# Order of the first loads, the second token tile's turn, and the first chunk's bias seed in a gated SSM and MLP kernel

## The chip, the cores and the metric

The kernel runs on one core of one Trainium2 chip. The metric is the device time of an execution in microseconds (us). Every execution is listed with its span (first to last instruction, about 1.8 us less than its time); each kernel leaves one profiled execution. Verdicts compare fast executions only: one that is over 1.5% above the fastest of the same kernel is called slow. Each interval is a 95% interval.

## The reference, cut to what matters

```python
x = A_x                                           # 2048 tokens x 640
g = sigmoid((x * gate_w).sum(-1, keepdims=True))
a = ssm(x, ...)                                   # a complex diagonal scan over the tokens
b = gelu(x @ w1 + b1) @ w2 + b2                   # 640 -> 1728 -> 640
out = g * a + (1 - g) * b
```

The kernel takes the tokens in four chunks of 512, each of four tiles of 128. The argument is about the first chunk's `x @ w1`, before everything else can start.

## The kernel before: the parts that matter

```python
load_x0(nc.sync, 0, 1, 0, KA * P)       # token tile 0, first 256 of 640 columns, 64 KB
load_w1a(nc.scalar, 0)                  # "strip 0": rows 0..127 of w1, 768 columns, 192 KB
load_x0(nc.sync, 1, 2, 0, KA * P)
load_w1a(nc.scalar, 1)
load_x0(nc.sync, 2, 3, 0, KA * P)
load_x0(nc.sync, 3, 4, 0, KA * P)
load_w1a(nc.sync, 2)
# ... then, all on SyncE: two transposing loads (columns 256..639), strips 4 and 3, the rest
for n in (512, 512, 512, 512, 512, 128, 128, 128, 128):     # warm-up, L237
    nc.tensor.matmul(pA[:, 0:n], lhsT=ones(P), rhs=ones(n), start=True, stop=True)

def turn_first(a, other):               # TensorE turns a token tile against an identity (L240)
    t = bank()                          # one of 8 PSUM banks
    turn(t, 0, a, 0)
    turned(nc.vector, t, 0, a, 0, 1)    # evict to SBUF (L247 DVE, L249 ScalarE)
    turn(other, a * P, a, 1)
    turned(nc.scalar if a else nc.vector, other, a * P, a, 1, 2)

turn_first(0, pA)
# ...
banks = [bank() for _ in range(FA)]     # 6 banks, one per 128 columns of a strip
# ... three filler matmuls (L363), then part(kd, a) = six 128-column matmuls (L278):
#     strip kd x token tile a, accumulated in the six banks
strip(0, 0, P, True, 0, FA // 2)
turn_first(1, pA)
strip(0, 0, P, True, FA // 2, FA)
part(1, 0)
turn_first(2, pA)
part(0, 1)
part(1, 1)
turn_first(3, pA)
part(0, 2)
# ... part(1,2), part(0,3), part(1,3), then strip 2 (256 columns at a time), strip 4, strip 3 (512)

def last_bank(c):                       # the last 65 columns, seeded with their bias
    p = bank()
    pv = p[:, 0:TPC * NL].rearrange("p (a n) -> p a n", a=TPC)
    if c == 0:
        nc.tensor.matmul(pv, lhsT=ident[:], rhs=b1x..., start=True, ...)     # L294
        return p, pv
    nc.scalar.activation(out=pv, in_=b1x..., func=ACT.Identity)              # L297
    act(0.4)
    return p, pv
```

## Time and profile before

| | before |
|---|---|
| time, median of the first three executions | 215.36 us |
| span of the profiled execution, a fourth one of 214.71 us | 212.9 us |
| TensorE (PE) busy | 208.7 us, 98% |
| DVE / ScalarE busy | 183.5 us / 101.7 us |

The span is one long TensorE stretch. So two things can shorten it: less TensorE work, or an earlier pass through the opening, in which TensorE waits for loads and evictions. The prediction shows the lines.

### The profile page before, as it was taken

Reading aid. Unit: us, or ns where it says so; the run is one execution under the profiler, and the core shown is the slowest. Engines: PE = TensorE matmul, PEld = TensorE weight load, DVE = VectorE, ACT = ScalarE, POOL = GpSimd, SP = SyncE. Lnnn points to the kernel's source line nnn. Section 1 sums busy time; section 2 is a strip of 40 time slices with the busy share of each in tenths; the row PEclk is TensorE's granted clock in tenths of the full one; section 3 lists DMA queues with packets and bytes.
Section 4 is the critical chain, followed back from the end, with each engine's and each line's share of the span. In section 5 each row is a group of like instructions: output and inputs, shape, how many; then the busy total and the mean of one; then the engine's idle time right before and its main releaser. Section 6 shows DMA issues by size and latency. Waiting matters only on the chain.

```text
span 212.9 us, 3594 instructions
## 1 busy us (share of the span) xinstructions
PE 208.7 (98%) x1372; PEld 125.2 (59%) x1383; DVE 183.5 (86%) x336; ACT 101.7 (48%) x182; POOL 62.7 (29%) x101
## 2 busy tenths in 40 slices
PE   8999999999999999999999999999999999999994
PEld 5745444454576644774457777444457587676773
DVE  2589999999989999999999999999999999903153
ACT  3599856665868587203653210456682422205100
POOL 7034079764432462404235503145000000000000
PEclk9999999999999999999999999999999999999999
DMA  6999999996000000061000005100000000100011
GB/s 176 228 218 214 191 237 313 300 211 167 3 0 0 3 0 0 12 186 65 0 0 3 0 20 167 62 0 0 0 5 14 0 3 31 62 34 0 0 66 62
DMA packets 33314, 16.24 MB, mean 76 GB/s; under 512 B 24720, under 2 KB 33296, under 8 KB 33296
## 3 DMA queue, kind: packets, MB, share of 16 engines
q1 hardware_dynamic: 32704, 15.57, 29.1%
q10 hardware_dynamic: 432, 0.43, 0.6%
q8 instruction: 11, 0.18, 0.4%
q14 instruction: 7, 0.06, 0.1%
q0 software_dynamic: 160, 0.01, 0.1%
HBM read 7.48 MB, written 2.62 MB: 47 GB/s over the span
## 4 chain that ended last, share of the span: by engine, by line
PE 97%; DMA 1%; issue 0%; DVE 0%
PE bank L608 27%; PE bank L278 26%; PE bank L667 20%; PE bank L551 20%; DMA xn<-in_A_x_dram 1%; PE bank L624 1%; PE bank L304 1%; PE bank L240 0%; DVE ot L672 0%; PE bank L363 0%; PE bank L294 0%; PE bank L393 0%; PE bank L376 0%
## 5 line engine op out<-in xcount | busy, mean ns | idle before, releaser
L608 PE MATMUL bank<-w_sb,gel 128*128 128x384 bf16 (+1 forms) x416 | 57.9, 299 | 0.0
L608 PEld LDWEIGHTS <-gel 128*128 128x128 bf16 x416 | 40.3, 98 | 17.0 <-issue 0.8
L554 ACT ACTIVATE bu<-bank 128x512 bf16<-128x512 f32 x40 | 23.6, 597 | 37.6 <-PE bank L551 37.6
L283 ACT ACTIVATE gel<-bank,colB 128x512 bf16<-128x512 f32 x52 | 34.0, 693 | 11.0 <-PE bank L278 10.8
L667 PEld LDWEIGHTS <-hs 128*128 128x128 bf16 x330 | 31.7, 98 | 11.6
L515 POOL TENSOR_SCALAR e<-g,cq 128x2 f32<-128x2 bf16 x15 | 18.3, 1222 | 64.3 <-DVE g L508 64.3
L508 DVE TENSOR_TENSOR_SCAN g<-r_c,carry,v 128x512 bf16<-128x512 f32 x30 | 37.2, 1271 | 0.0
L616 ACT ACTIVATE gb<-bank,gcol 128x384 f32<-128x384 f32 (+1 forms) x32 | 15.1, 525 | 33.9 <-PE bank L624 16.9
L278 PE MATMUL bank<-xT,w1a 128*128 128x512 bf16 (+2 forms) x158 | 27.2, 325 | 0.2
L667 PE MATMUL bank<-CT_re,hs 128*128 128x320 bf16 (+2 forms) x165 | 27.1, 295 | 0.0
L667 PE MATMUL bank<-CT_im,hs 128*128 128x320 bf16 (+2 forms) x165 | 27.1, 295 | 0.0
L672 DVE SCALAR_TENSOR_TENSOR ot<-bank,gcol,gb 128x320 bf16<-128x320 f32 (+2 forms) x33 | 17.4, 533 | 9.6 <-PE bank L667 9.5
L551 PE MATMUL bank<-xT,BT_im 128*128 128x512 bf16 x99 | 24.8, 379 | 0.1
L551 PE MATMUL bank<-xT,BT_re 128*128 128x512 bf16 x97 | 24.5, 379 | 0.2
L278 PEld LDWEIGHTS <-w1a 128*128 128x128 bf16 x162 | 14.1, 99 | 11.8
L582 DVE TENSOR_TENSOR bank<-xn,Dbc 128x320 f32<-128x320 bf16 (+2 forms) x33 | 14.5, 483 | 7.1 <-ACT gb L616 7.1
L278 PE MATMUL bank<-xT,w1b 128*128 128x512 bf16 x80 | 17.9, 379 | 0.0
L551 PEld LDWEIGHTS <-BT_im 128*128 128x128 bf16 x100 | 9.8, 98 | 11.8
L517 POOL TENSOR_TENSOR carry<-e,e 128x1 f32<-128x1 f32 x30 | 15.8, 547 | 1.3
L551 PEld LDWEIGHTS <-BT_re 128*128 128x128 bf16 x100 | 9.6, 98 | 11.0
L489 DVE TENSOR_TENSOR v<-wa,wb 128x512 bf16<-128x512 bf16 x40 | 15.2, 422 | 0.6
L597 ACT ACTIVATE bank<-b2bc 128x384 f32<-128x384 bf16 (+1 forms) x24 | 11.7, 529 | 7.1 <-DVE ot L672 7.1
(112 smaller groups left out, 215.8 us busy)
## 6 DMA issues: line engine op xcount, KB each, us to landing
out_dram<-ot SPq DMA_DIRECT2D x15, 160.0 KB, 1.8
w_sb<-in_B_w_dram SPq DMA_DIRECT2D x2, 640.0 KB, 6.0
xn<-in_A_x_dram SPq DMA_DIRECT2D x2, 640.0 KB, 4.3
w_sb<-in_B_w_dram SPq DMA_DIRECT2D x1, 800.0 KB, 8.8
w1b<-in_B_w_dram SPq DMA_DIRECT2D x5, 128.0 KB, 3.4
xn<-in_A_x_dram SPq DMA_DIRECT2D x4, 160.0 KB, 2.8
w1a<-in_B_w_dram SPq DMA_DIRECT2D x3, 192.0 KB, 3.1
w1a<-in_B_w_dram ACTq DMA_DIRECT2D x2, 192.0 KB, 3.0
```

Of the source, the lines that this page charges most:

```text
L278: nc.tensor.matmul(p[:, t0:t1], lhsT=w, rhs=xT[c][:, kd, t0:t1], start=(kd == 0) if first is None else first, stop=(kd == last), skip_grou ...
L283: nc.scalar.activation(out=gel[c][:, kf, :], in_=p[:, :], func=ACT.Gelu_apprx_tanh, bias=b1_c[:, kf:kf + 1])
L489: nc.vector.tensor_tensor(out=o, in0=a, in1=b, op=op)
L508: nc.vector.tensor_tensor_scan(s["g"][:, ri, :], r_c[:, ks:ks + 1].to_broadcast([P, CH]), s["v"][:, ri, :], init, ALU.mult, ALU.add)
L515: nc.gpsimd.tensor_scalar(out=t[:], in0=g[:, :, CH - 1], scalar1=f[:, ks:ks + 1], scalar2=None, op0=ALU.mult)
L517: nc.gpsimd.tensor_tensor(out=carry[:, ri, ks:ks + 1], in0=m[0][:, ri:ri + 1], in1=m[1][:, 1 - ri:2 - ri], op=op)
L551: nc.tensor.matmul(p[:], lhsT=BT[ks >= KSA][:, kd, (ks % KSA if ks < KSA else ks - KSA) * P:][:, 0:P], rhs=xT[c][:, kd, :], start=(kd == 0 ...
L554: nc.scalar.activation(out=bu[:, ri, :], in_=p[:], func=ACT.Identity)
L608: nc.tensor.matmul(p[:, col:col + d1 - d0], lhsT=gel[c][:, kf, a * P:(a + 1) * P], rhs=w2_sb[:, kf, d0:d1], start=False, stop=False, skip_ ...
L616: nc.scalar.activation(out=gbs[ti][:, d0:d1], in_=p[:, col:col + d1 - d0], func=ACT.Identity, scale=gcol[:, 1, ti:ti + 1])
L667: nc.tensor.matmul(p[:, 0:d1 - d0], lhsT=hs[c][:, j, lo:lo + P], rhs=CT[:, j % KS, d0:d1], start=False, stop=(j == 2 * KS - 1), skip_group ...
L672: nc.vector.scalar_tensor_tensor(out=ot[:, d0:d1], in0=p[:, 0:d1 - d0], scalar=gcol[:, 0, ti:ti + 1], in1=gbs[ti][:, d0:d1], op0=ALU.mult, ...
```

## The change

It means to bring the second token tile in together with the first, so that both are turned while TensorE would otherwise wait for an eviction, and to take one matmul off TensorE.

```diff
     load_x0(nc.sync, 0, 1, 0, KA * P)
-    load_w1a(nc.scalar, 0)
-    load_x0(nc.sync, 1, 2, 0, KA * P)
+    load_x0(nc.scalar, 1, 2, 0, KA * P)
+    load_w1a(nc.sync, 0)
     load_w1a(nc.scalar, 1)
-    load_x0(nc.sync, 2, 3, 0, KA * P)
     load_x0(nc.sync, 3, 4, 0, KA * P)
+    load_x0(nc.scalar, 2, 3, 0, KA * P)
     load_w1a(nc.sync, 2)
...
-    def turn_first(a, other):
-        t = bank()
+    def turn_first(a, other, t=None):
+        t = t or bank()
...
-        turned(nc.scalar if a else nc.vector, other, a * P, a, 1, 2)
+        turned(nc.scalar, other, a * P, a, 1, 2)
...
-        if c == 0:
-            nc.tensor.matmul(pv, lhsT=ident[:], rhs=b1x[:]... , start=True, stop=True, ...)
-            return p, pv
...
+    turn_first(1, banks[FA - 1], banks[FA - 2])
     # (three fillers)
-    strip(0, 0, P, True, 0, FA // 2)
-    turn_first(1, pA)
-    strip(0, 0, P, True, FA // 2, FA)
+    part(0, 0)
+    part(0, 1)
     part(1, 0)
     turn_first(2, pA)
-    part(0, 1)
     part(1, 1)
     turn_first(3, pA)
```

Lines move: L277, L299, L359 and L292 of the changed kernel are L278, L304, L363 and L297 of the one before.

More of the change, by code (lines that the diff above doesn't have):

```diff
@@ L292, in last_bank @@
         pv = p[:, 0:TPC * NL].rearrange("p (a n) -> p a n", a=TPC)
-        if c == 0:
-            nc.tensor.matmul(pv, lhsT=ident[:], rhs=b1x[:].rearrange("p (o n) -> p o n", o=1).to_broadcast([P, TPC, NL]),
-                             start=True, stop=True, skip_group_check=True)
-            return p, pv
         nc.scalar.activation(out=pv, in_=b1x[:].rearrange("p (o n) -> p o n", o=1).to_broadcast([P, TPC, NL]), func=ACT.Identity)
```

## The prediction

> **What bounds the kernel now.** I read the page's busy shares first, then its chain of waits, then the chain of the first 20 us in order of time, then the timeline of the first 9 us engine by engine. The page:
>
> ```profile
> PE 208.7 (98%) x1372; PEld 125.2 (59%) x1383; DVE 183.5 (86%) x336; ACT 101.7 (48%) x182; POOL 62.7 (29%) x101
> PE 97%; DMA 1%; issue 0%; DVE 0%
> ```
>
> TensorE is busy for 98% of the span and is 97% of the chain that ends last. DVE, at 86%, has slack: its last `hs` write is at 184.6 us and TensorE starts to read those at 199.2. So a change helps only as far as it takes work off TensorE or lets TensorE get through its opening sooner. Everything that the change moves lies in the opening (before 20 us). The chain there (start, length, what):
>
> ```profile
> 0.72 2.76 DMA xn<-in_A_x_dram
> 3.48 0.05 issue
> 3.53 0.40 PE bank L240 x2
> 3.93 0.32 PE bank L363 x3
> 4.25 0.44 PE bank L278 x3
> 4.68 0.21 PE bank L240 x2
> ...
> 9.15 1.89 PE bank L278 x8
> 11.04 0.01 PE bank L393
> 11.05 6.05 PE bank L278 x28
> 17.11 0.11 PE bank L294
> ```
>
> 2.76 us go to the first token tile's load. From 3.53 us there is always a TensorE piece. L240 turns a token tile, L363 are three filler matmuls, L278 are the strips of the first product, and L294 is the bias seed that the change takes away: 0.11 us of chain. The transfers and evictions behind it (start, length, engine):
>
> ```profile
> 0.72 0.90 ACTq L126 DMA_DIRECT2D w1a<-in_B_w_dram  x2
> 0.72 1.83 SPq L135 DMA_DIRECT2D xn<-in_A_x_dram  x4
> 1.65 1.28 ACT L147 ACT_TABLE_LOAD   x1 [1.65 <-PEq L725]
> 2.60 0.43 SPq L126 DMA_DIRECT2D w1a<-in_B_w_dram  x1
> 3.07 2.65 SPq L150 DMA_TRANSPOSE xT<-in_A_x_dram  x2
> 5.76 1.06 SPq L126 DMA_DIRECT2D w1a<-in_B_w_dram  x2
> ```
>
> Each plain issue takes about 0.47 us of SyncE (four in 1.83 us, with gaps of 0.05), a transpose 1.3. Adding each issue's time to landing to its start gives landings of 3.48 (tile 0), 3.67 (strip 0), 3.86 (tile 1), 4.26 (strip 1), 4.90 (tile 2), 5.70 (tile 3), 6.04 (strip 2), 7.58 (first transpose) and 8.88 (strip 4). Two details of TensorE's records matter. First, its clock: twelve matmuls start in 3.53 to 4.90 us and 44 in the 2.30 us after; successive starts of 128-column matmuls lie 0.107 us apart before 4.90 and 0.056 after. Work that is pulled ahead of 4.90 counts half. Second, two hand-overs further on are set by loads: the first 256-column strip starts at 7.625, 0.127 after the matmul before it instead of 0.056 (the transpose landed at 7.58), and strip 4's weights are loaded at 8.918, just after their landing at 8.88, where TensorE was ready at 8.93. **A gain in the first 4 us is worth nothing unless strip 4 also lands earlier.**
>
> **What the Trainium skill says.** (1) "TensorE: Matmul & The Clock Gate", Part 1: the array starts at half rate and opens after some 4 us of activity (plus or minus 0.5 us), with starts 107 and 56 ns apart. The trace agrees: 0.107 and 0.056, changing at 4.90 us, 4.1 after the first matmul. (2) "DMA: Bandwidth & Descriptors", "Queues, rings and completion order": each DMA engine takes turns between the queues at packet granularity. The packets of the first 3.5 us fit: those of tile 0 (512 bytes, 27 ns each) and of strip 0 (1536 bytes, 65 ns) run interleaved on the two queues. (3) Same page, "Issuing engines are not separate DMA queues": a second issuing engine saves issue time only. So the reorder can bring a transfer forward, but not add bandwidth. (4) "ScalarE: Activation LUTs", "What ACT_TABLE_LOAD costs": 186 ns + 0.833 per column with immediate operands, 403 ns for 260 columns; the trace's three other seeds took 380 to 383 ns.
>
> **Part by part.**
>
> *Loads.* Both queues now open with a token tile. An engine has 8 packets of each (128 rows over 16 engines). Tile 0 shared its turns with strip 0: 8 x (27+65) = 0.74 us; now with tile 1: 8 x (27+27) = 0.43. Tile 0 should land 0.3 us earlier, near 3.2, tile 1 with it (before 3.86). Then strips 0 and 1 share the turns, 8 x (65+65) = 1.04 us, and land together. The four transfers are the same bytes as before, when the last of them landed at 4.26, so I put strip 0 at about 4.2 (before 3.67): **later by half a microsecond.** SyncE issues four loads, not five, ahead of the transposes, so the transposes and strip 4 are issued 0.47 us sooner. DMA engines are about 95% occupied by then, so I expect 0.3 to 0.5 us of it: first transpose near 7.2, strip 4 near 8.5.
>
> *TensorE to 7.2 us.* The warm-up matmuls end at about 3.28 (last start 3.17 + 0.107), which caps the earlier start: turns from 3.28, not 3.53. Four turns and three fillers at 0.107 reach 4.03; the eviction behind the first strip (0.33 from matmul to DVE, 0.29 on DVE, 0.05 hand-over) is ready at 3.95 and hidden, where before it was exposed (3.93 + 0.107 to 4.20 leaves 0.16). The first strip then waits for its weights to about 4.25. By 4.90 that gives 7 + 6.1 = 13.1 matmuls against 12. A lead of 1.1 matmuls is 1.1 x 0.056 = **0.06 us**. With the weights at 4.0 it would be 3 matmuls, 0.17; with 4.4, none.
>
> *Transposes.* If the first lands near 7.2, the **0.07 us** stall at 7.55 goes too; strip 4 is then wanted at 8.80 and lands near 8.5.
>
> *ScalarE.* One more issue pushes its table load from 1.65 to about 2.1; the warm activation ends at 3.6, ahead of its first eviction (about 3.72). Tile 1's second bank is emptied by 4.3, and the sixth strip wants it only at 4.7. DVE has one eviction less.
>
> *Seed.* TensorE loses L294, **0.11 us** from chain (260 columns at 2.4 columns a ns). ScalarE gains 0.38 us here:
>
> ```profile
> 16.79 2.47 ACT L283 ACTIVATE gel<-bank,colB 128x512 bf16<-128x512 f32 x4
> 19.42 0.69 ACT L283 ACTIVATE gel<-bank,colB 128x512 bf16<-128x512 f32 x1 [0.16 <-PE bank L278]
> ```
>
> It works back to back up to 19.26 with 0.16 us to spare. The instruction order puts the seed after the third of the four, so it runs at about 18.5 to 18.9; TensorE needs it at 19.21 - 0.11 - 0.13 = 18.97. That fits by 0.1 us. What follows on ScalarE comes some 0.2 us later, but DVE first needs it at 27.4, and the copies that feed it ended at 23.3.
>
> Sum: 0.06 + 0.07 + 0.11 = 0.24 us, and nothing later takes it back because no TensorE wait shows after 9 us. 215.36 - 0.24 = **215.1 us**.
>
> **Rivals.** *The second token tile buys a wait for strip 0.* If strip 0 lands at 4.5 or later, the head gains nothing and loses about 0.1; only the seed is left: 215.3 to 215.4. For it: strip 0 is now behind two loads and shares with strip 1. Against: the same bytes were in by 4.26. *The head is gained but given back at strip 4.* If its landing stays at 8.88 because the DMA engines are full, everything before 8.93 is lost and the seed alone counts: 215.25. For it: zero slack at 8.93 now. Against: strip 4 is set by issue order (3.1 us from issue to landing), and the transfers move 111 GB/s at 6.8 to 7.3 us, against 278 at 4.8 to 5.3, so the engines are not full of data there. *ScalarE becomes the wait at the first chunk's last tile.* A seed that ends at 19.1 rather than 18.9 gives back 0.1 to 0.2. *All goes well:* strip 0 by 4.0 as well, 0.35 us, 215.0.
>
> **Range and chances.** All of these lie within 0.4 us. The three runs before differ by 0.3, and the clock gate's moment can move by a few tenths. I take 214.75 to 215.5. Two per cent would be 4.3 us, ten times what the opening holds: chances 0.01 faster, 0.98 same, 0.01 slower.
>
> **What would show it.** Tile 0 landing near 3.2 and the first turn at 3.3; first strip near 4.25 with its weights the last to come; starts at 0.107 spacing still up to about 4.9; first 256-column strip with no gap, 0.1 us sooner; strip 4's weights ahead of need; no L294 matmul, and the 65-column matmuls of the first chunk with no gap ahead of them, about 0.24 us sooner than 19.21. A first strip after 4.5, a strip 4 still at 8.9, or a gap before those matmuls would each make the sum wrong by the size given.

## The result, and the profile after

Ratios here are the mean time of one kernel's fast executions over that of the other's of the same rounds, so they are not quite the ratios of the medians that stand beside them. All outputs are right.

In the first measurement the changed kernel took **214.71 us** (median of six, 214.45 to 214.92) and the one before 215.26 us (median of six, 214.71 to 215.46): ratio 0.9976, interval 0.9962 to 0.999. The prediction had 215.1 and 214.75 to 215.5. So the gain was more than twice the 0.24 us foreseen, and the time fell just below the range.

The two profiles do not show such a gain: their spans are 212.93 and 212.80 us (executions of 214.71 and 214.58 us). The page of the changed kernel, its busy line and its chain's:

```profile
PE 208.9 (98%) x1382; PEld 125.0 (59%) x1382; DVE 183.2 (86%) x335; ACT 102.0 (48%) x184; POOL 62.7 (29%) x101
PE 97%; DMA 2%; SPq 0%; DVE 0%; issue 0%
```

(The profile before lacks some ten matmul records, so the counts can't be compared.) The bound is what it was. In the chain of the first 22 us, start and length first, the DMA now waited for is another one:

```profile
1.18 3.30 DMA w1a<-in_B_w_dram
4.48 0.05 issue
4.52 1.18 PE bank L277 x18
5.70 0.11 PE bank L240 x2
5.82 0.34 PE bank L277 x6
6.15 0.27 PE bank L240 x2
```

Before, 2.76 us went to tile 0, and strips began at 4.20. Now the chain comes from strip 0, and strips begin at 4.52, later. The timeline of the same stretch of the changed kernel shows two waits:

```profile
3.27 0.63 PE L240 MATMUL bank<-ident,xn 128*128 128x128 bf16 x4
3.70 0.49 PE L359 MATMUL bank<-const-bfloat16-1.0 128*128 128x128 bf16 x3
4.52 1.18 PE L277 MATMUL bank<-xT,w1a 128*128 128x128 bf16 x18 [0.34 <-DMA w1a<-in_B_w_dram]
5.54 0.28 PE L240 MATMUL bank<-ident,xn 128*128 128x128 bf16 x2
5.65 0.50 PE L277 MATMUL bank<-xT,w1a 128*128 128x128 bf16 x6
5.80 0.29 DVE L247 CAST xT<-bank 128x128 bf16<-128x128 f32 x1 [1.67 <-PE bank L240]
6.14 0.27 PE L240 MATMUL bank<-ident,xn 128*128 128x128 bf16 x2
```

The turns start at 3.27, as soon as the warm-up is over. But after the fillers TensorE has nothing to do until strip 0 lands at 4.48. And there is a wait that nobody had foreseen: the turn of tile 3 (L240 at 6.14) starts 0.21 us after the matmul before it, where a warm start is 0.056 us later. The turn is released by the end of DVE's eviction of tile 2, which runs from 5.80 to 6.09. By the order of the `bank()` calls both tiles are turned in the same PSUM bank; the trace itself leaves bank numbers out. The profile's wait column says nothing there, because pipelined matmul records overlap the gap; it is seen by taking the differences of successive starts.

Strip 4 lands at 8.60 instead of 8.88 and starts at 8.93, as before. So in these two executions the opening is worth nothing, and all but 0.01 of the 0.13 us between them is the seed. The first chunk's end before (L294 is the seed matmul) and after (ScalarE's seed is L292):

```profile
16.94 0.28 PE L294 MATMUL bank<-b1x,ident 128*128 128x260 bf16 x1
17.06 0.81 PE L278 MATMUL bank<-xT,w1c_lo 128*128 128x512 bf16 x3
19.21 0.26 PE L304 MATMUL bank<-w1c_lo,xT 128*128 128x65 bf16 x3
```

```profile
18.56 0.47 ACT L292 ACTIVATE bank<-b1x 128x260 f32<-128x260 bf16 x1
19.09 0.26 PE L299 MATMUL bank<-w1c_lo,xT 128*128 128x65 bf16 x3
```

The seed ends at 19.03; the 65-column matmuls that need it start at 19.09, 0.12 us earlier than before (19.21) and with no gap ahead of them.

### The profile page after: what moved, and what is told of

It reads as the page before. It is cut to its first block, busy times and chain, and to the rows that moved or that the text cites. A ratio compares the mean times of both kernels' runs of the same rounds, so it can differ in the third digit from the quotient of the medians.

```text
span 212.8 us, 3603 instructions
## 1 busy us (share of the span) xinstructions
PE 208.9 (98%) x1382; PEld 125.0 (59%) x1382; DVE 183.2 (86%) x335; ACT 102.0 (48%) x184; POOL 62.7 (29%) x101
## 4 chain that ended last, share of the span: by engine, by line
PE 97%; DMA 2%; SPq 0%; DVE 0%; issue 0%
PE bank L602 27%; PE bank L277 27%; PE bank L661 20%; PE bank L545 20%; DMA w1a<-in_B_w_dram 2%; PE bank L618 1%; PE bank L299 1%; SPq L135 0%; PE bank L240 0%; DVE ot L666 0%; PE bank L387 0%; PE bank L370 0%
## 5 line engine op out<-in xcount | busy, mean ns | idle before, releaser
L277 PE MATMUL bank<-xT,w1a 128*128 128x512 bf16 (+2 forms) x162 | 27.0, 324 | 0.3 <-DMA w1a<-in_B_w_dram 0.3
L277 PEld LDWEIGHTS <-w1a 128*128 128x128 bf16 x162 | 13.8, 98 | 12.2 <-DMA w1a<-in_B_w_dram 0.6
L277 PE MATMUL bank<-xT,w1b 128*128 128x512 bf16 x80 | 17.9, 379 | 0.0
```

The lines of the kernel that those rows point to most:

```text
L277: nc.tensor.matmul(p[:, t0:t1], lhsT=w, rhs=xT[c][:, kd, t0:t1], start=(kd == 0) if first is None else first, stop=(kd == last), skip_grou ...
```

## The experiments

**The question.** Where do 0.55 us come from, when one profile against the other shows 0.13? Theory H: the opening of the kernel before usually goes slower than in its one profile. Theory S: the extra time lies later. A third possibility was plain scatter.

**1 and 2. Both kernels again.**

> The kernel before, unchanged, timed against itself, to see how far its executions differ among themselves (214.71 to 215.46 us in six) and to get a second profile of it. Theory H (the head): its one profile fell on a fast execution (span 212.93 us), and the usual one is some 0.5 us longer because the opening goes slower; a profile with a span near 213.4 then has its first strip-4 weights after 8.93 us by the same 0.5 us. Theory S (later stages vary): the opening reads as before, strip 4 at 8.9, and the extra time lies after 20 us. Ratio 1.000 within 0.0015 under both.

Measured: 215.06 us (with the slow one; 214.96 without) beside 214.97 us for the same kernel, ratio 0.9999 (0.9982 to 1.0017). Its executions spread from 214.56 to 215.50, except one that took 449 us. The profile fell on that one; it is slow and is not compared with anything (more at the end). So this run decides nothing between the theories; 12 below repeats it.

> The changed kernel again, for a tighter interval. If the first measurement holds: 0.45 to 0.6 us less (0.9972 to 0.998). If scatter: 0.1 to 0.3 us less (0.9986 to 0.9995). The two parts (e_seed and e_head) should add up to it within 0.1 us.

Measured: 214.76 us beside 214.97, ratio 0.9995 (0.9975 to 1.0016). The first measurement did not hold. The profiled execution took 215.82 us, 1.2 us more than the profiled one of the first measurement, from the same code on a healthy core. Its timeline:

```profile
4.69 2.10 PE L277 MATMUL bank<-xT,w1a 128*128 128x128 bf16 x18 [0.46 <-DMA w1a<-in_B_w_dram]
6.58 0.36 PE L240 MATMUL bank<-ident,xn 128*128 128x128 bf16 x2
6.78 0.50 PE L277 MATMUL bank<-xT,w1a 128*128 128x128 bf16 x6
7.27 0.27 PE L240 MATMUL bank<-ident,xn 128*128 128x128 bf16 x2
```

The same eighteen strip matmuls take 2.10 us here and 1.18 above. Their starts are 0.107 us apart and drop to 0.056 only at 6.8 us: the array's clock opened there and not before 4.6. Together with a strip 0 that landed 0.16 us later, that is where 1.1 us went. The wait of 0.21 us ahead of tile 3's turn is there again.

**3 and 4. The two halves of the change.**

```diff
 e_seed = before, less:
-        if c == 0:
-            nc.tensor.matmul(pv, lhsT=ident[:], rhs=b1x[:]..., start=True, stop=True, ...)
-            return p, pv
 e_head = the changed kernel, with these lines put back
```

> The kernel before with one part of the change alone: the first chunk's bias seed by ScalarE, no seed matmul. All theories that take the seed at its chain length expect 0.11 us less (ratio 0.9995) and the 65-column matmuls of the first chunk without a gap ahead of them. A rival, that the seed matmul costs more than its chain length and carries the gain of 0.55 us, expects 0.4 us less or more (0.998).

> The changed kernel with the seed matmul put back: the new load order and the new TensorE order alone. Theory H expects 0.3 to 0.45 us less than before (0.998 to 0.9985), about all of what was measured less 0.11. If the 0.55 us was mostly scatter of the six runs, 0.0 to 0.13 us less (0.9994 to 1.000), as the two profiles show at strip 4 (8.93 in both).

Measured: e_seed 214.82 us, ratio 0.9988 (0.9973 to 1.0002); e_head 215.22 us, ratio 1.0010 (0.9994 to 1.0027). So the loads and the new order alone gain nothing that shows; if anything they lose. The two parts add up to -0.06 us by the means, against -0.11 for the whole change beside the same executions, within the 0.1 expected but also within the noise. The rival that the seed matmul costs 0.4 us or more is not settled by these times, but it is by the profiles: the span less the start of strip 4 is the same number in every profile with TensorE's seed (204.00, 204.01, 203.99, 203.99 and 204.01 us in the kernel before, e_head, e_loads, a later repeat of the kernel before, and e_nowarm) and another in every one with ScalarE's (203.87 to 203.91 us in eight). **The seed is worth 0.11 us (the difference of the two means), and all other differences among these thirteen executions have arisen by the time strip 4 starts.** That rules out theory S for them.

The trace of e_seed also shows the other limit of the opening. Its clock was open by 4.1 us, and TensorE was ready for strip 4 at 8.61 (its last matmul of strip 2 starts at 8.505 and takes 0.109), but strip 4 landed at 9.20. The weight loads there:

```profile
8.29 0.21 PEld L278 LDWEIGHTS <-w1a 128*128 128x128 bf16 x2
9.24 0.33 PEld L278 LDWEIGHTS <-w1a 128*128 128x128 bf16 x3 [0.75 <-DMA w1a<-in_B_w_dram]
```

An early clock is thus cut off by strip 4's landing in the load order of before (8.88, 9.20, 8.83 in three fast profiles). In the new order it lands at 8.17 to 8.61 and no longer cuts anything off.

**5. The clock.** If the clock's moment makes the scatter, moving it must move the time.

```diff
 e_nowarm = before, less:
-    for n in (512, 512, 512, 512, 512, 128, 128, 128, 128):
-        nc.tensor.matmul(pA[:, 0:n], lhsT=ones(P), rhs=ones(n), start=True, stop=True)
```

> The kernel before without its nine warm-up matmuls: TensorE first works at 3.5 us and not at 0.76. Theory G (gate): executions of one kernel differ because the array's clock opens at another moment each time (4.1 to 6.8 us in five profiles, 3.4 to 6.1 after the first matmul), and every microsecond of delay costs half a one. Then the clock here opens 2.7 us later, at 6.9 or after, and the time rises by 0.7 to 1.4 us: ratio 1.003 to 1.0065, strip 4 after 10 us. Rival: the spread comes from the loads alone; then nothing changes but noise, 0.999 to 1.0015.

Measured: 215.91 us beside 214.86, ratio 1.0049 (1.0025 to 1.0072). In the profile TensorE's first matmul is at 3.17 us, the clock opens at 7.58, and strip 4 starts at 9.93 (expected: after 10). Its lines, with strips that stay slow, and then the line of before:

```profile
5.51 1.48 PE L276 MATMUL bank<-xT,w1a 128*128 128x128 bf16 x12
7.00 1.42 PE L276 MATMUL bank<-xT,w1a 128*128 128x128 bf16 x18
```

```profile
5.41 0.83 PE L278 MATMUL bank<-xT,w1a 128*128 128x128 bf16 x12
```

Twelve strips took 1.48 us; twelve in the profile of before, with the clock open, 0.83. The loads landed about as in the kernel before (strip 0 at 3.31, strip 4 at 9.13), so the rival that the loads alone move the time, which expected 0.999 to 1.0015, is out.

**6. The new load order alone.**

```diff
 e_loads = before, with the six load lines of the changed kernel
```

> The kernel before with the new load order alone; TensorE order, evictions and seed as before. Token tile 0 lands near 2.9, strip 0 at 4.3 to 4.6, so the first strip starts half a microsecond later than before and the warm TensorE time between is lost; strip 4 lands at 8.2 to 8.6 and no longer holds TensorE when the clock opens early. By my model of the opening the two cancel: 1.000 within 0.001. If the later strip 0 is what matters, 1.001 or more; if strip 4 is, 0.999 or less.

Measured: 215.10 us beside 214.86, ratio 1.0010 (0.9997 to 1.0023), at the upper edge of "the two cancel". In the profile tile 0 landed at 2.87, strip 0 at 4.57 and strip 4 at 8.47. TensorE went through the turns and the fillers at full clock (it opened at 3.5 here, the earliest seen) and then waited from 3.64 to 4.61 us, in the end for strip 0. Even with the earliest clock of all, strip 4 started only at 9.00.

**7. The wait for the bank.**

```diff
 e_turn = the changed kernel, with
     part(0, 1)
-    part(1, 0)
     turn_first(2, pA)
+    part(1, 0)
     part(1, 1)
     turn_first(3, pA)
```

> The changed kernel with tile 2 turned one part earlier, so that twelve strips and not six lie between the turns of tiles 2 and 3. Theory B (bank): in all three profiles of the changed head the turn of tile 3 starts 0.21 us after the matmul before it, because its bank is the one that tile 2 was just turned in, and DVE has to empty it first. Then this wait is gone here (0.056 or 0.107 apart) and the time falls by 0.15 us against the changed kernel: ratio to before 0.998 to 0.9990. Rival: that wait is the landing of tile 3 (4.84 to 5.13 us, so a second too early for it) or is made up later; then the wait or the time stays, 0.999 to 1.000.

Measured: 214.88 us beside 214.86, ratio 1.0003 (0.9988 to 1.0018). The profile confirms the theory: tile 2 is turned at 5.27, tile 3 at 6.05, 0.056 us after the matmul before it.

```profile
5.27 0.28 PE L240 MATMUL bank<-ident,xn 128*128 128x128 bf16 x2
6.05 0.28 PE L240 MATMUL bank<-ident,xn 128*128 128x128 bf16 x2
```

The rival cause falls too: tile 3 landed at 4.95 here, as it had with the wait (the "second too early" of the expectation means a microsecond). The time does not confirm the 0.15 us: the ratio missed the 0.998 to 0.9990 expected, and its interval is wider than the effect. What the wait costs is read from the starts (0.154 us in each of the four profiles that have it), not from the times.

**8 and 9. Strip 0 sooner.**

```diff
 e_fast, e_fast2 = e_turn, with
     load_x0(nc.scalar, 1, 2, 0, KA * P)
     load_w1a(nc.sync, 0)
-    load_w1a(nc.scalar, 1)
-    load_x0(nc.sync, 3, 4, 0, KA * P)
     load_x0(nc.scalar, 2, 3, 0, KA * P)
+    load_w1a(nc.sync, 1)
+    load_x0(nc.scalar, 3, 4, 0, KA * P)
     load_w1a(nc.sync, 2)
```

> As e_turn, and strip 1 goes behind strip 0 on SyncE's queue, while ScalarE's carries tiles 1, 2 and 3: strip 0 then shares the engines' turns with a token tile and not with strip 1. By packet counts 8 x (65+27) = 0.74 us in place of 1.04: strip 0 should land at 4.0 to 4.25 (4.27 to 4.64 in the three profiles of the new load order), the first strip start there, and the time fall 0.05 to 0.2 us below e_turn: ratio 0.9975 to 0.9987. If strip 0's landing is set by its issue or by latency and not by sharing, it stays at 4.3 to 4.6 and the time equals e_turn.

> e_fast again, as the candidate that may beat both kernels: by my model 0.16 us earlier at strip 4 than before on average, and 0.12 of seed: 0.28 us less, ratio 0.9980 to 0.9995. Its profile has tile 3's turn with no wait of 0.2 us ahead.

Measured: 214.57 us beside 214.86, ratio 0.9985 (0.9969 to 1.0000), and 214.60 us beside 214.99, ratio 0.9989 (0.9972 to 1.0005). Strip 0 landed at 4.30 in the first profile (outside the 4.0 to 4.25 expected) and at 3.87 in the second (earlier than expected). So what sets its landing in this order is not settled. The second has the shortest span of the profiles, 212.45 us:

```profile
3.70 0.53 PE L359 MATMUL bank<-const-bfloat16-1.0 128*128 128x128 bf16 x3
4.02 1.04 PE L277 MATMUL bank<-xT,w1a 128*128 128x128 bf16 x12
```

TensorE goes from the fillers straight into the strips, as the change had meant it to; the clock opened at 4.5.

**10. Keep strip 0 first, and free SyncE.**

```diff
 e_mix = e_seed, with
-    load_x0(nc.sync, 3, 4, 0, KA * P)
+    load_x0(nc.scalar, 3, 4, 0, KA * P)     # behind strip 1
```

> The kernel before, with its TensorE order, strip 0 still first on ScalarE's queue and the first two tiles on SyncE's; only tile 3's load moves from SyncE's queue to ScalarE's, behind strip 1, and the seed is ScalarE's. Theory M: what the change gained in the opening is the earlier issue of the transposes and of strip 4 (one load fewer ahead of them on SyncE), and what it lost is the later strip 0; so this keeps the gain without the loss. Strip 0 lands at 3.5 to 3.7, the first strip starts at 4.1 to 4.2, the first transpose lands at 6.9 to 7.2 and strip 4 at 8.2 to 8.6; by my model, averaged over the moments at which the clock opens, strip 4 starts 0.18 us earlier than before, and with the seed 0.30 us less in all: ratio 0.9981 to 0.9991. If the transfers are limited by bandwidth, strip 4 stays at 8.8 to 9.2 and only the seed's 0.12 us is left: 0.9994.

Measured: 214.67 us beside 214.99, ratio 0.9986 (0.9974 to 0.9998). Strip 0 landed at 3.43, the first strip started at 3.97, strip 4 landed at 8.43 and started at 8.79. One part of the expectation missed: the first transpose landed at 7.44, not 6.9 to 7.2, and tile 2 only at 5.05, so TensorE waited 0.36 us for it (its clock was open by 4.0). This kernel keeps the order of before and needs one moved line and the seed; it does as well as e_fast within the scatter. It was measured once, in five executions; the first measurement of the change also had an interval without 1, and did not hold.

**11 and 12. More executions.**

> The changed kernel a third time, to put the 0.55 us of the first measurement against the scatter. If the opening's clock decides it by chance, the mean of all its executions less that of all of before tends to -0.1 to -0.3 us (ratio here 0.998 to 1.0005), the profile again shows the wait of 0.21 us ahead of tile 3's turn, and its strip 4 starts where my model puts it for the moment at which the clock opened (8.9 up to 4.5 us, 9.13 at 5, 9.6 at 6, 9.9 at 6.8) within 0.1. If the first measurement was right: 0.997 to 0.998.

> The kernel before once more, against itself: the scatter of a ratio that should be 1, and another moment of the clock. Ratio within 0.002 of 1. Strip 4 starts at 8.8 to 9.25 if the clock opened before 5 us (then set by strip 4's landing), at 9.35 for 6 and 9.73 for 6.8, within 0.15; the span is that start plus 204.0 us.

Measured: the changed kernel 214.70 us beside 214.99, ratio 1.0003 (0.9978 to 1.0028; one execution of 216.47 pulls the mean up); the kernel before 214.95 us, ratio 1.0003 (0.9991 to 1.0015). The changed kernel's clock opened by 4.7 and its strip 4 started at 9.08, with strip 0 landing at 4.63 and 0.21 us ahead of tile 3's turn. In the repeat of before the clock opened at 5.7 and strip 4 started at 9.14, within the 0.15 expected, with strip 0 landing at 3.41. Theory H is right in part: the opening of before was 0.2 us slower here than in its first profile, whose execution (214.71 us) is 0.25 below the median of all.

**What the profiles say together.** All times in us from the start of the span; "by" means that TensorE stood idle while the clock opened:

| profile | first strip | clock opens | strip 4 starts | span | span less strip 4's start |
|---|---|---|---|---|---|
| before | 4.20 | 4.9 | 8.93 | 212.93 | 204.00 |
| before, repeated | 3.97 | 5.7 | 9.14 | 213.14 | 203.99 |
| e_seed | 4.11 | by 4.1 | 9.24 (its landing) | 213.13 | 203.89 |
| changed | 4.52 | by 4.6 | 8.93 | 212.80 | 203.87 |
| changed, second repeat | 4.68 | by 4.7 | 9.08 | 212.97 | 203.89 |
| changed, first repeat | 4.69 | 6.8 | 10.05 | 213.95 | 203.89 |
| e_head | 4.31 | 6.0 | 9.46 | 213.47 | 204.01 |
| e_turn | 4.56 | by 4.7 | 8.85 | 212.72 | 203.87 |
| e_fast, e_fast2 | 4.35, 4.02 | 5.3, 4.5 | 9.01, 8.54 | 212.89, 212.45 | 203.88, 203.91 |
| e_mix | 3.97 | by 4.0 | 8.79 | 212.67 | 203.88 |
| e_loads | 4.61 | 3.5 | 9.00 | 212.99 | 203.99 |
| e_nowarm | 3.85 | 7.6 | 9.93 | 213.94 | 204.01 |

I wrote the opening down as a sum: the matmuls in their order, each at 0.107 or 0.056 us per 128 columns, and the landings, evictions and the bank as lower bounds. With each profile's own landings and clock it gives the start of strip 4 within 0.04 us in eleven fast profiles; e_mix and e_nowarm I did not run through it. With the clock's moment spread evenly over 3.45 to 6.85 us, the range seen but an assumed spread, it gives an estimate of the change's average: the opening loses 0.1 us, the seed gains 0.11, and together the two kernels are level. For a clock at 4.5 the change gains 0.07 + 0.11 us, for one at 6 it loses 0.26 - 0.11. A second such sum, built separately from the same traces, came within 0.07 us in all thirteen and has the opening lose 0.12 us on average.

Over all fast executions the kernel before has a median of 214.96 us and a mean of 215.00 (49 of them), the changed one 214.71 and 214.87 (18). The difference is 0.25 us by the medians and 0.13 by the means, the latter with a standard error of 0.13. Executions of the kernel before spread over 1.1 us (214.56 to 215.68). In the second sum a clock at 6.8 in place of 3.5 us costs 0.8 us there and 1.0 in the changed kernel, so the clock's moment accounts for most of such a spread. The changed kernel's longest, 216.47 us, was not profiled and is 0.65 us above the one with the clock at 6.8; its cause is open.

## Why the prediction was right or wrong

- *What bounds the kernel, and that only the opening and the seed can matter*: right. DVE took nothing back, and no TensorE wait appeared after strip 4.
- *Seed, 0.11 us*: right, 0.11 measured. The tight fit at the chunk's end held with 0.06 us to spare, though the seed took 0.47 us on ScalarE and not 0.38.
- *Tile 0 near 3.2*: it landed at 2.75 to 2.96 in the six profiles with the new order. That the warm-up caps the gain at 3.27 was right, so the surplus bought nothing.
- *Strip 0 "at about 4.2"*: this term failed. It landed at 4.27 to 4.64 in the six (changed and its repeats 4.48, 4.64, 4.63; e_head 4.27, e_loads 4.57, e_turn 4.51), though "the same bytes were in by 4.26": the last of these four loads, strip 1, came at 4.56 to 4.90. I had divided a fixed sum of packets and assumed that the engines stay full. They don't: between 2.6 and 3.0 us the two token tiles are almost in, the strips' data has hardly begun, and 15 to 131 GB/s move, against 261 to 346 in the four fast profiles that load strip 0 first with the old queue order (e_nowarm, e_seed, the kernel before twice). That this hole alone makes the lateness is argued from its size. Nor is it shown that two loads take turns packet by packet, as the sum of 8 x (65+65) has it: the trace doesn't tell which of the 16 engines moved a packet. The views by stretch, before and then after (busy TensorE, clock, share of the DMA engines, GB/s):

```profile
2.60:3.00 0.40, 0.40 (x4) 1.00 1.03 346
```

```profile
2.60:3.00 0.40, 0.40 (x4) 1.00 0.85 131
```

- *"By 4.90 that gives 7 + 6.1 = 13.1 matmuls against 12", 0.06 us*: failed with it. First strips started at 4.3 to 4.7, not 4.25. The first rival's wait, for a strip 0 that lands at 4.5 or later, came true in four of the six.
- *"Nothing later takes it back"*: failed inside the opening. Only six strips lie between the turns of tiles 2 and 3 in the new order, 0.34 us, and the bank that they share needs 0.6 us to be turned into and emptied; in the old order twelve lie between. The order of instructions showed it, but of the banks the prediction followed only tile 1's. It costs 0.154 us per execution.
- *Transposes and strip 4 earlier by 0.3 to 0.5 us*: right for strip 4, in part for the first transpose, which landed at 6.98 to 7.50 in the same six profiles against 7.23 to 7.58 in the four of the old order. Strip 4 landed at 8.17 to 8.61 in the same six profiles against 8.83 to 9.20. The stall of 0.07 us ahead of strip 2 was gone too in the changed kernel's three profiles. The earlier strip 4 is all that the opening gained, and it pays only where the clock opens early.
- *The base of 215.36 us, and "the three runs before differ by 0.3, and the clock gate's moment can move by a few tenths"*: this is the step that put the measured time outside. The base is the median of three executions, and all 49 fast ones have 214.96: it was 0.4 us high. 214.96 - 0.24 = 214.72 is what the changed kernel then took, each time (medians 214.71, 214.76, 214.70). So by the medians it was the kernel before that was drawn high in the first measurement, 215.26 where later ones gave 214.86 to 214.99, and 0.30 of the 0.55 us is that draw. By the means both were drawn, the changed kernel low (214.69, its twelve later executions 214.96) and the other high (215.20, later 214.97). There was a sign of it: the profile that I read had taken 214.71 us, 0.65 less than the base from which I subtracted; its span of 212.9 us and the usual 1.8 say the same. The range was too narrow for the same reason. The moment moves by 3.3 us (3.5 to 6.8), each worth up to half, and six executions do not average that out.
- *The size, 0.24 us*: it agrees with the medians of all executions (0.25), but by luck. Of its three terms the seed's 0.11 held; the stall of 0.07 went, and the 0.06 at the head never came; the later strip 0 and the bank took from the opening what the transfers gave it.

What stays open: the average gain of the opening is below what these timings resolve (the difference of the means less the seed is 0.02 us, with a standard error of 0.13; the estimate has a loss of 0.1), and how the clock's moment is really spread is known only from twelve profiles. Why the clock opens when it does, no run tests.

## What to carry to other kernels

Before you explain a fraction of a per cent, find out what the same code scatters by and why: here it is the moment at which TensorE's clock opens, and a second profile of the kernel before would have shown it before any theory was needed. Subtract a gain from the time of the execution whose profile you read, or from many executions, not from three others. When you reorder an opening, follow each buffer as well as each transfer: two uses of one PSUM bank must lie an eviction apart. And moving a small load forward moves a large one back; what brought strip 4 forward was not the tile that came first but the issue slot that was freed ahead of it, as e_mix shows with one moved line.

## What the Trainium skill lacked or had wrong

- "TensorE: Matmul & The Clock Gate", Part 1, gives the transition as about 4 us, plus or minus 0.5 us from run to run. With the first matmul at 0.76 us in each, the profiles have it between 3.5 and 6.8 us, so 2.7 to 6.0 us after. The same section says that the window of 3.4 us runs freely, which fits the measured spread of 3.3 us; the half microsecond does not. Between two profiled executions of the changed kernel, strip 4's start differed by 1.1 us, most of it from this.
- The same section warns that clock events in a trace have been seen to be unreliable, but shows no case. Here the profile's granted-clock column reads 1.00 for stretches in which 128-column matmuls start 0.107 us apart (3.5 to 4.9 us of the kernel before) as for those at 0.056. Here only the starts show it.
- The same section reports a clock stuck at a quarter for 50 us and more. What happened here is longer and less deep, and may be something else. One of 49 + 1 executions of the kernel before took 449 us: throughout its span of 447 us, 512-column matmuls started mostly 0.44 to 0.56 us apart instead of 0.216, while DVE and ScalarE kept their pace. The cause is open.
- "DMA: Bandwidth & Descriptors", "Issuing engines are not separate DMA queues", calls the issue time that a second engine saves usually small relative to the transfer. In this opening a place in the queue mattered: strip 0 issued second, 0.46 us after its queue's first transfer, landed at 3.87 to 4.64 us in eight profiles, against 3.31 to 3.67 in five in which it was issued first. How much of that is the later issue, how much the sharing with strip 1 or a tile, and how much the slow start of the transfers (15 to 131 GB/s at 2.6 to 3.0 us) the runs do not separate. No page has this gap.
- "ScalarE: Activation LUTs", "What ACT_TABLE_LOAD costs": its 403 ns for a 260-column activation lies between the 0.38 us of three seeds in the kernel before and the 0.47 us of the first chunk's in all eight profiles that have it.
